# A Fourier mixer and a mixture of experts in one kernel: x loaded once per tile, and the first three batches' filter product without an exchange of rows on ScalarE

## The chip, the core and the metric

The kernel runs on one core of a Trainium2 chip. The metric is the device time of one execution in microseconds; the kernel before was timed three times.

## What is computed

The input x has 8 batches of 2496 tokens of 256 numbers, all in float32. Each batch is transformed along the tokens, multiplied by a complex filter, and transformed back. The result goes, token by token, to one of eight experts (the largest of eight logits), each with two matrices.

```python
X = np.fft.rfft(x, axis=1)
F = (filt_r + 1j * filt_i)[None, :, :]
y = np.fft.irfft(X * F, n=x.shape[1], axis=1)
x = y.reshape(B * S, D)
expert_idx = np.argmax(x @ w_gate, axis=1)
for e in range(E):
    h = np.maximum(x_sorted[lo:hi] @ w1[e], 0.0)
    y_sorted[lo:hi] = h @ w2[e]
return gate_w[:, None] * y_sorted[inv_perm]
```

## The kernel before, in words

The length 2496 is 39 times 64, so a transform is taken in stages, each a set of small matrix products on TensorE. For each batch:

- `add_x` (L378, L379): of a loaded tile of x, the sum `xs` of two halves and, in place, their difference. The sum is on GpSimd (POOL in the profile), the difference on VectorE (DVE) in batch 0 and on GpSimd in all others.
- Stage a (`stage_a`, L389; in batch 0 `first_a`, L472): the transform over 39, in six chunks. The result goes to DRAM (`zd`) and comes back in another layout as five tiles `z` (in batch 0 it stays on the core and is turned by TensorE, `turn_z`, L485).
- Stage b (`stage_b`, L403): the transform over 64. Its result lies in two PSUM banks `po`, with real parts in some rows and imaginary parts in others. Then the filter: VectorE makes `ys = po * hr` (L408), ScalarE (ACT) copies `po` to `yw` with the rows exchanged in blocks of 32, eight copies (L410), VectorE multiplies `yw` by `hi` (L411), and GpSimd adds the two (L412). `hi` carries signs that GpSimd puts into it once (L283).
- Stage c (`stage_c`, L424; in batch 0 `first_c`, L495): the way back over 64, from `ys`. The result goes to DRAM (`ud`) and comes back as tiles `u`.
- Stage d (`stage_d`, L445), the logits (L533) and `route`, which writes each token's row by an indirect DMA from GpSimd (L649), 22 per batch in groups of eight, eight and six, to a place that its expert owns.

The experts' tiles (`hidden`, L787, and `result`, L801) take those rows when enough are there, and fill TensorE between the stages and to the end.

The program is written as one list. `slot(k)` lists the steps of a slot: stages b and c of batch k, `add_x` and stage a of batch k+1, and stage d and routing of batch k-1. Each step has a place in its slot, a planned cost on TensorE and, where it needs one, the tile that has to be loaded. The loop at the end takes steps and expert work in turn, by these costs. `either` gives a copy out of PSUM to VectorE or ScalarE, whichever is planned free first. Every engine then works in the order in which its instructions were written; all loads and stores but the indirect ones stand in one queue, SyncE's (SP).

What is loaded, and in which order, comes from the steps too:

```python
todo = [step[2] for step in STEPS if step[2] and step[2] != "y"]
```

Both `add_x` and stage a of a chunk name the same tile of x, so each tile of x stands in `todo` twice and is loaded twice, into two of the seven buffers named `fin`.

Of the kernel before, what the change touches and what calls it, by code (L numbers as in the profile page):

```python
# [19 lines left out]
P = 128  # L20
# [37 lines left out]
def dft_tables():  # L58
# [29 lines left out]
    tc = tc.reshape(2, N2, N2)  # L88
    tc0 = np.zeros((2, N2, 2, 2, N2))
    for e in range(2):  # L90
        tc0[e, :, :, e] = tc.transpose(1, 0, 2)
# [13 lines left out]
    for e in range(2):  # L105
# [6 lines left out]
        "tc": np.concatenate([tc, tc], axis=1).transpose(1, 0, 2),  # L112
        "tc0": tc0.reshape(P, 2, P),
# [40 lines left out]
def kernel(  # L154
# [64 lines left out]
    tcs = cst.tile([P, 2, N2], F32, name="tcs")  # L219
# [20 lines left out]
    tc0 = pro.tile([P, 2, P], F32, name="tc0", bufs=1)  # L240
# [32 lines left out]
    HP = P // 2  # L273
    CH = [(i0, min(4, NG - i0)) for i0 in range(0, NG, 4)]
# [97 lines left out]
    def add_x(b, c):  # L372

        m = CH[c][1] // 2
        xt = ins["x", b, c]
        xs = xss[b, c] = sb.tile([TP, 2, D], F32, tag="xs", name="xs", bufs=2)
        lo, hi_ = xt[:TP, :m], xt[:TP, m:2 * m]
        nc.gpsimd.tensor_tensor(xs[:, :m], lo, hi_, op=ALU.add)  # L378
        (nc.vector if b == 0 else nc.gpsimd).tensor_tensor(hi_, lo, hi_, op=ALU.subtract)  # L379
        free["p"] = max(free["p"], now[0]) + (1.3 if b == 0 else 2.6)  # L380
# [15 lines left out]
    def stage_b(b, q):  # L396
# [9 lines left out]
        yw = sb.tile([P, 2, 2 * D], F32, tag="yw", name="yw", bufs=2)  # L406
        for o in range(2):
# [9 lines left out]
    def stage_c(b, q):  # L417
        ys = outs.pop(("y", b, q))
        uo = sb.tile([P, 4, D], F32, tag="st", name="uo", bufs=4)
        pe = [bank(), bank()]  # L420
        for o in range(2):
            for e in range(2):
                rows = slice(e * HP, (e + 1) * HP)
                mm(pe[e][o * HP:(o + 1) * HP, :], lhsT=tcs[rows, o, :], rhs=ys[rows, o, :], start=True, stop=True)  # L424
# [64 lines left out]
    def first_c(q):  # L489
        ys = outs.pop(("y", 0, q)).rearrange("p o (j d) -> p o j d", j=2)  # L490
        for h in range(DH):
            p = bank().rearrange("p (j o x) -> p j o x", j=2, o=2)
            for j in range(2):
                for o in range(2):
                    mm(p[:, j, o], lhsT=ys[:, o, j, h * P:(h + 1) * P], rhs=tc0[:, o, :], start=True, stop=True)  # L495
# [55 lines left out]
    def route(b, g):  # L551
# [13 lines left out]
        oh = small("oh", w, E)  # L565
# [42 lines left out]
        run = small("run", E, w, rows=P)  # L608
# [6 lines left out]
        pos = small("pos", E, w)  # L615
# [203 lines left out]
    def slot(k):  # L819

        steps, nch = [], len(CH)
        if k == 0:
            steps.append((0.4, load_rest, None, 0.0))
            for q in range(-1, NQ + 1):
# [58 lines left out]
    todo = [step[2] for step in STEPS if step[2] and step[2] != "y"]  # L883
# [145 lines left out]
```

## Time and profile before

| | |
|---|---|
| median of 3 runs | 1778.66 us (1776.59 to 1780.38) |
| the profiled execution | 1764.16 us |
| its span, first to last instruction | 1762.4 us |
| TensorE matmuls | 1577.6 us busy, 90% of the span |
| TensorE weight loads | 1059.7 us, 60% |
| ScalarE | 635.0 us, 36% |
| GpSimd | 556.2 us, 32% |
| VectorE | 458.3 us, 26% |

The profile is of one execution. Busy shares are means over stages with different limits, so they are read by stretches of time. A pass is one matmul as the trace records it: each float32 matmul of the program is two passes.

### The profile page before, as it was taken

The numbers are of one execution on the slowest core, as the hardware profiler recorded it, in microseconds if no ns is written. First come the engines' busy times: TensorE is split into PE (matmuls) and PEld (weight loads), VectorE is DVE, ScalarE is ACT, GpSimd is POOL, SyncE is SP. The second block draws the span as 40 slices with busy tenths as digits, with TensorE's granted clock in tenths as the row PEclk, the third lists the DMA queues.
The fourth block names the chain that finished last, engine by engine and source line by source line (L and its number), as shares of the span: only waits on it lengthen the run. The fifth ranks groups of instructions, "written<-read, shape, count | busy, mean of one in ns | idle before, by whom it ended". The sixth has DMA issues, their size and how long they took to land.

```text
span 1762.4 us, 22497 instructions
## 1 busy us (share of the span) xinstructions
PE 1577.6 (90%) x7058; PEld 1059.7 (60%) x7058; DVE 458.3 (26%) x1490; ACT 635.0 (36%) x1382; POOL 556.2 (32%) x498
## 2 busy tenths in 40 slices
PE   6785657579987989999997999999999999999998
PEld 4441224248552656565662675666767668889998
DVE  3554455531344421421124312111300000000000
ACT  3454443343453422533235433222222222223333
POOL 5535444444344342521223323112511111111111
PEclk9787668789997989999998999999999999999999
DMA  9457866486978264863537436333444445665561
GB/s 368 154 157 226 232 226 206 131 270 205 267 259 253 87 232 137 244 193 110 151 97 180 153 110 182 122 105 112 146 152 160 149 143 186 198 231 157 179 182 57
DMA packets 139238, 313.27 MB, mean 178 GB/s; under 512 B 21871, under 2 KB 62992, under 8 KB 139121
## 3 DMA queue, kind: packets, MB, share of 16 engines
q1 hardware_dynamic: 119905, 268.50, 49.8%
q0 software_dynamic: 19216, 43.33, 7.2%
q8 instruction: 58, 0.95, 0.2%
q14 instruction: 59, 0.48, 0.1%
HBM read 231.75 MB, written 80.90 MB: 177 GB/s over the span
## 4 chain that ended last, share of the span: by engine, by line
PE 72%; ACT 3%; DVE 3%; DMA 2%; issue 2%; POOL 2%; SPq 0%; POOLq 0%; DVEq 0%; ACTq 0%
PE bank L801 31%; PE bank L787 30%; ACT yw L410 3%; PE bank L445 2%; PE bank L780 2%; PE bank L389 2%; PE bank L519 1%; PE lt L533 1%; PE bank L403 1%; POOL rows L649 1%; DMA fin<-in_x_dram 1%; PE bank L424 1%; DMA w2t<-in_moe_w_dram 1%; DVE ys L408 0%; POOL xs L378 0%
## 5 line engine op out<-in xcount | busy, mean ns | idle before, releaser
L787 PE MATMUL bank<-xT,w1t 128*128 128x512 f32 (+2 forms) x2080 | 597.2, 441 | 17.0 <-issue 13.3
L801 PE MATMUL bank<-w2t,hT 128*128 128x256 f32 x2240 | 496.5, 380 | 2.1 <-ACT yw L410 1.3
L787 PEld LDWEIGHTS bank<-xT,w1t 128*128 128x128 f32 x2080 | 341.8, 193 | 242.7 <-issue 209.6
L801 PEld LDWEIGHTS bank<-w2t,hT 128*128 128x128 f32 x2240 | 421.1, 190 | 65.9 <-issue 6.6
L807 POOL DMA_INDIRECT out_dram<-ys,idt x163 | 161.2, 989 | 790.6 <-ACT ys L806 438.5
L791 ACT ACTIVATE hT<-bank 128x512 f32<-128x512 f32 (+2 forms) x500 | 217.1, 436 | 337.7 <-PE bank L787 337.5
L806 ACT ACTIVATE ys<-bank,gts 128x256 f32<-128x256 f32 x155 | 73.4, 474 | 491.4 <-PE bank L801 445.4
L649 POOL DMA_INDIRECT rows<-yo,row x176 | 176.5, 1003 | 171.3 <-DVE cnt L630 73.1
L410 ACT COPY yw<-bank 32x512 f32<-32x512 f32 x320 | 184.3, 576 | 100.5 <-DVE ys L408 96.7
L266 DVE COPY xT<-bank 128x512 f32<-128x512 f32 (+2 forms) x60 | 28.3, 475 | 543.6 <-PE bank L780 451.7
L412 POOL TENSOR_TENSOR ys<-ys,yw 128x1024 f32<-128x1024 f32 x40 | 94.0, 2349 | 171.1 <-DVE yw L411 126.8
L389 PE MATMUL bank<-xs,tas 117*120 117x512 f32 (+1 forms) x84 | 48.9, 668 | 67.7 <-POOL xs L378 38.7
L411 DVE TENSOR_TENSOR yw<-yw,hi 128x1024 f32<-128x1024 f32 x40 | 51.5, 1287 | 167.3 <-ACT yw L410 150.3
L801 PE MATMUL bank<-w2s,hT 128*128 x368 | 83.3, 379 | 0.0
L445 PE MATMUL bank<-fin,tds 120*117 120x512 f32 (+1 forms) x154 | 78.8, 631 | 0.1
L378 POOL TENSOR_TENSOR xs<-fin 117x512 f32<-117x512 f32 (+1 forms) x48 | 56.6, 1180 | 58.2 <-PE bank L389 31.1
L801 PEld LDWEIGHTS bank<-w2s,hT 128*128 128x128 f32 x368 | 68.2, 190 | 8.3
L408 DVE TENSOR_TENSOR ys<-bank,hr 128x512 f32<-128x512 f32 x80 | 51.4, 684 | 80.3 <-PE bank L403 78.7
L424 PE MATMUL bank<-ys,tcs 64*64 64x512 f32 x280 | 42.5, 680 | 30.3 <-POOL ys L412 30.3
L389 PEld LDWEIGHTS bank<-xs,tas 117*120 117x120 f32 x84 | 14.9, 208 | 85.8 <-POOL xs L378 71.6
L449 DVE TENSOR_TENSOR yo<-bank,even 117x256 f32<-117x256 f32 x88 | 37.1, 422 | 75.7 <-ACT even L448 73.2
L519 PEld LDWEIGHTS bank<-ident,yo 117*128 117x128 f32 x352 | 41.1, 150 | 25.1 <-issue 16.2
(134 smaller groups left out, 1092.7 us busy)
## 6 DMA issues: line engine op xcount, KB each, us to landing
w1t<-in_moe_w_dram SPq DMA_DIRECT2D x130, 512.0 KB, 3.9
w2t<-in_moe_w_dram SPq DMA_DIRECT2D x84, 512.0 KB, 4.8
fin<-in_x_dram SPq DMA_DIRECT2D x80, 512.0 KB, 6.0
fin<-zd SPq DMA_DIRECT2D x140, 128.0 KB, 5.2
ud<-uo SPq DMA_DIRECT2D x140, 128.0 KB, 3.0
zd<-zo SPq DMA_DIRECT2D x70, 240.0 KB, 5.6
fin<-ud SPq DMA_DIRECT2D x70, 240.0 KB, 5.8
xg<-rows SPq DMA_DIRECT2D x28, 544.0 KB, 4.6
```

The costliest lines, as they stand in the source:

```text
L389: mm(p, lhsT=tas, rhs=v, start=True, stop=True)
L410: nc.scalar.copy(out=yw[r:r + HB, o], in_=po[o][r ^ HB:(r ^ HB) + HB])
L412: nc.gpsimd.tensor_tensor(ys, ys, yw, op=ALU.add)
L424: mm(pe[e][o * HP:(o + 1) * HP, :], lhsT=tcs[rows, o, :], rhs=ys[rows, o, :], start=True, stop=True)
L445: mm(p[:TP, :], lhsT=tds[:k, :], rhs=uv[:, i], start=True, stop=True)
L519: nc.tensor.transpose(pt[:, 2 * i + dh, :TP], yo[:, j + i, dh * P:(dh + 1) * P], ident[:TP, :TP])
L649: sc = nc.gpsimd.indirect_dma_start(out=rowsd, out_offset=bass.IndirectOffsetOnAxis(ap=at, axis=0), in_=what, in_offset=None,)
L787: mm(p[:, :m], lhsT=w1t[2 * i + k // FH2][:, dh, k % FH2 * P:(k % FH2 + 1) * P], rhs=xts[i][:, dh, :m], start=(dh == 0), stop=(dh == DH - 1))
L791: lambda: nc.scalar.activation(hT[:, :m], p[:, :m], AF.Relu))
L801: mm(p[:, :D], lhsT=hs[i][k][:, j * P:(j + 1) * P], rhs=w2, start=(k == 0), stop=(k == FT - 1))
L806: lambda: nc.scalar.activation(ys, p[:, :D], AF.Copy, scale=gate))
L807: nc.gpsimd.indirect_dma_start(out=out, out_offset=bass.IndirectOffsetOnAxis(ap=idt[i].bitcast(U32)[:, j, :], axis=0), in_=ys, in_offset=None,
```

## The change

It does three things, and leaves batches 3 to 7 as they were but for the loads and one place in the list.

- `todo` keeps each tile once, so x is loaded 48 times, not 96.
- In batches 0 to 2 (`EARLY = 3`), `add_x` is on VectorE whole. In every batch its place in the list moves from 0.1 to 0.05 of a slot ahead of stage a.
- In batches 0 to 2, stage b's result is multiplied twice by VectorE, `ys = po * hr` and `yw = po * hi`, without any exchange; stage c then takes both products into the same PSUM bank, with two matrices, the second being the first with its two halves of rows exchanged and its sign turned. ScalarE's eight copies, VectorE's multiplication of `yw`, and GpSimd's addition are gone there.

```diff
+    tc = np.stack([tc, -tc[:, ::-1]], axis=1).reshape(2, 2, N2, N2)
...
+    EARLY = 3
...
-        nc.gpsimd.tensor_tensor(xs[:, :m], lo, hi_, op=ALU.add)
-        (nc.vector if b == 0 else nc.gpsimd).tensor_tensor(hi_, lo, hi_, op=ALU.subtract)
-        free["p"] = max(free["p"], now[0]) + (1.3 if b == 0 else 2.6)
+        eng = nc.vector if b < EARLY else nc.gpsimd
+        eng.tensor_tensor(xs[:, :m], lo, hi_, op=ALU.add)
+        eng.tensor_tensor(hi_, lo, hi_, op=ALU.subtract)
...
+        if b < EARLY:
+
+            for o in range(2):
+                for y, h in ((ys, hr), (yw, hi)):
+                    nc.vector.tensor_mul(y[:, o], po[o], h[:, q, 2 * o:2 * o + 2].rearrange("p j d -> p (j d)"))
+            outs["w", b, q] = yw
+            free["v"] = max(free["v"], now[0]) + 2.8
+            return
...
-                mm(pe[e][o * HP:(o + 1) * HP, :], lhsT=tcs[rows, o, :], rhs=ys[rows, o, :], start=True, stop=True)
+                for i, y in enumerate(parts):
+                    mm(pe[e][o * HP:(o + 1) * HP, :], lhsT=tcs[rows, o, i, :], rhs=y[rows, o, :],
+                       start=(i == 0), stop=(i == len(parts) - 1))
...
-                    mm(p[:, j, o], lhsT=ys[:, o, j, h * P:(h + 1) * P], rhs=tc0[:, o, :], start=True, stop=True)
+                    for i, y in enumerate(parts):
+                        mm(p[:, j, o], lhsT=y[:, o, j, h * P:(h + 1) * P], rhs=tc0[:, o, i, :], start=(i == 0), stop=(i == 1))
...
-                    steps.append((at + 0.02, lambda q=q: first_c(q - 1), None, 1.7))
+                    steps.append((at + 0.02, lambda q=q: first_c(q - 1), None, 3.4))
...
-                    steps.append((at + 0.01, lambda q=q: stage_c(k, q - 1), None, 0.95))
+                    steps.append((at + 0.01, lambda q=q: stage_c(k, q - 1), None, 1.8 if k < EARLY else 0.95))
...
-                steps.append((at - 0.1, lambda c=c: add_x(k + 1, c), ("x", k + 1, c), 0.0))
+                steps.append((at - 0.05, lambda c=c: add_x(k + 1, c), ("x", k + 1, c), 0.0))
...
-    todo = [step[2] for step in STEPS if step[2] and step[2] != "y"]
+    todo = list(dict.fromkeys(step[2] for step in STEPS if step[2] and step[2] != "y"))
```

The routing's small tiles `oh`/`run` and `ex`/`pos` now share buffers, which makes room for the larger matrices.

How the order of instructions moves, at three places. First SyncE's queue at the start of the program, before:

```order
L964 DMA tas<-in_ta_dram 117x120
L355 DMA fin<-in_x_dram 128x1024 x9
L355 DMA fin<-in_x_dram 128x512
L355 DMA fin<-in_x_dram 128x1024
L355 DMA fin<-in_x_dram 128x512
L355 DMA fin<-in_x_dram 128x1024
L279 DMA sgs<-in_sg_dram 128x20
```

and now:

```order
L982 DMA tas<-in_ta_dram 117x120
L358 DMA fin<-in_x_dram 128x1024 x5
L358 DMA fin<-in_x_dram 128x512
L358 DMA fin<-in_x_dram 128x1024
L282 DMA sgs<-in_sg_dram 128x20
L283 DMA tbs<-in_tb_dram 128x64
```

Thirteen loads of x stood ahead of the filter's tables; seven do now.

Second, VectorE in batch 0, around stage b's first two tiles (`zi`, `zo`, `ut` are copies out of PSUM), before:

```order
L408 TENSOR_TENSOR ys<-bank,hr 128x512 x2
L411 TENSOR_TENSOR yw<-yw,hi 128x1024
L266 COPY zi<-bank 128x512 x2
L266 COPY zo<-bank 120x512
L408 TENSOR_TENSOR ys<-bank,hr 128x512 x2
L411 TENSOR_TENSOR yw<-yw,hi 128x1024
```

and now:

```order
L418 TENSOR_TENSOR ys<-bank,hr 128x512
L418 TENSOR_TENSOR yw<-bank,hi 128x512
L418 TENSOR_TENSOR ys<-bank,hr 128x512
L418 TENSOR_TENSOR yw<-bank,hi 128x512
L382 TENSOR_TENSOR xs<-fin 117x512
L383 TENSOR_TENSOR fin<-fin 117x512
L418 TENSOR_TENSOR ys<-bank,hr 128x512
```

The multiplication that waited for ScalarE is gone, the copies that stood behind it went to ScalarE, and batch 1's sums stand between the products.

Third, GpSimd around batch 3's sums (`rows` are the indirect writes of batch 0's tokens), before:

```order
L412 TENSOR_TENSOR ys<-ys,yw 128x1024 x2
L378 TENSOR_TENSOR xs<-fin 117x512
L379 TENSOR_TENSOR fin<-fin 117x512
L649 DMA rows<-yo,row 160768x272 x7
L378 TENSOR_TENSOR xs<-fin 117x512
```

and now:

```order
L286 TENSOR_TENSOR hi<-hi,sgs 128x1024 x5
L667 DMA rows<-yo,row 160768x272 x8
L382 TENSOR_TENSOR xs<-fin 117x512
L383 TENSOR_TENSOR fin<-fin 117x512
L667 DMA rows<-yo,row 160768x272 x8
L382 TENSOR_TENSOR xs<-fin 117x512
```

Batch 3's first sum stands behind eight writes and its second behind eight more; no addition of `ys` and `yw` is left between them.

## Rows read from the trace of the kernel before

**Rows 1.** The page's first line.

```profile
span 1762.4 us, 22497 instructions
```

**Rows 2.** Windows: PE, PEld, DVE, ACT and POOL busy, granted clock, DMA share, GB/s.

```profile
0.00:24.40 24.40, 14.18 (x96) 13.47 (x96) 8.75 (x24) 5.94 (x14) 8.69 (x22) 1.00 0.91 333
24.40:81.00 56.60, 39.64 (x177) 23.61 (x177) 29.20 (x39) 27.75 (x47) 34.97 (x22) 0.81 0.60 219
81.00:163.50 82.50, 57.10 (x268) 25.84 (x271) 37.88 (x82) 41.44 (x81) 35.83 (x27) 0.79 0.64 194
163.50:255.80 92.30, 57.61 (x237) 23.98 (x229) 48.09 (x142) 41.85 (x86) 39.81 (x33) 0.70 0.75 228
...
1000.00:1762.40 762.40, 755.87 (x3540) 573.90 (x3538) 76.03 (x382) 227.94 (x567) 151.71 (x154) 1.00 0.48 152
```

**Rows 3.** Waits of PE, whole span: us in total, times, longest.

```profile
PE bank L389 <- POOL xs L378: 38.7, 7, 13.3
PE bank L424 <- POOL ys L412: 30.3, 6, 8.5
...
PE bank L403 <- DVE zi L266: 10.8, 4, 3.3
...
PE bank L495 <- POOL ys L412: 4.4, 1, 4.4
```

**Rows 4.** Timeline of PE, start and slot 0: start, us, instruction, idle before it.

```profile
9.56 2.06 PE L472 MATMUL bank<-tas,xs 117*128 117x120 f32 x8 [9.56 <-POOL seg L303]
...
33.49 2.57 PE L403 MATMUL bank<-zi,tbs 64*64 64x512 f32 x8 [3.34 <-DVE zi L266]
...
46.04 1.95 PE L495 MATMUL bank<-tc,ys 128*128 128x128 f32 x16
```

**Rows 5.** Timeline of VectorE, the product behind the exchange.

```profile
158.00 1.22 DVE L411 TENSOR_TENSOR yw<-yw,hi 128x1024 f32<-128x1024 f32 x1 [4.17 <-ACT yw L410]
```

**Rows 6.** Timeline of PE, slots 1 and 2.

```profile
120.82 1.03 PE L424 MATMUL bank<-ys,tcs 64*64 64x512 f32 x8
...
147.26 1.99 PE L424 MATMUL bank<-ys,tcs 64*64 64x512 f32 x8 [6.86 <-POOL ys L412]
...
150.18 1.06 PE L389 MATMUL bank<-fin,tas 117*120 117x256 f32 x2
...
161.79 1.98 PE L424 MATMUL bank<-ys,tcs 64*64 64x512 f32 x8 [8.52 <-POOL ys L412]
...
174.75 1.99 PE L424 MATMUL bank<-ys,tcs 64*64 64x512 f32 x8 [4.71 <-POOL ys L412]
176.66 3.04 PE L445 MATMUL bank<-fin,tds 120*117 120x512 f32 x4
184.35 2.06 PE L389 MATMUL bank<-xs,tas 117*120 117x512 f32 x2 [4.66 <-POOL xs L378]
...
204.42 2.06 PE L389 MATMUL bank<-xs,tas 117*120 117x512 f32 x2 [10.95 <-DMA ud<-uo]
```

**Rows 7.** Groups by line: operation, count, busy us, mean ns, idle before.

```profile
L408 DVE TENSOR_TENSOR ys<-bank,hr 128x512 f32<-128x512 f32 x80 | 51.4, 684 | 80.3 <-PE bank L403 78.7 <-issue 0.9 <-POOL xs L378 0.4
...
L379 DVE TENSOR_TENSOR fin<-fin 117x512 f32<-117x512 f32 (+1 forms) x6 | 4.4, 730 | 10.7 <-POOL xs L378 10.7
```

**Rows 8.** Stage c's line alone, 120.7 to 121.9 us: durations, first and last start.

```profile
L424 PE MATMUL bank<-ys,tcs x8: 589/590/591, 120.8 to 121.3; 64*64 64x512 f32 x8
```

**Rows 9.** Timeline of GpSimd in slot 2.

```profile
194.33 1.00 POOL L649 DMA_INDIRECT rows<-yo,row  x1 [8.68 <-DVE cnt L630]
...
203.09 1.27 POOL L378 TENSOR_TENSOR xs<-fin 117x512 f32<-117x512 f32 x1
```

**Rows 10.** DMA issues: count, KB each, median us to landing.

```profile
fin<-in_x_dram SPq DMA_DIRECT2D x80, 512.0 KB, 6.0
fin<-zd SPq DMA_DIRECT2D x140, 128.0 KB, 5.2
```

**Rows 11.** The chain that ended last, 420 to 700 us: start, us.

```profile
460.88 6.38 DMA fin<-in_x_dram
```

More of the change, by code (lines that the diff above doesn't have):

```diff
@@ L87, in dft_tables @@
         tc[o, 0, :, 1], tc[o, 1, :, 1] = sn.T, cs.T
-    tc = tc.reshape(2, N2, N2)
-    tc0 = np.zeros((2, N2, 2, 2, N2))
+    tc = np.stack([tc, -tc[:, ::-1]], axis=1).reshape(2, 2, N2, N2)
+    tc0 = np.zeros((2, N2, 2, 2, 2, N2))
     for e in range(2):
-        tc0[e, :, :, e] = tc.transpose(1, 0, 2)
+        tc0[e, :, :, :, e] = tc.transpose(2, 0, 1, 3)
     ids = np.zeros((NB, N1, NG))
@@ L111, in dft_tables @@
         "tb": tb.reshape(P, N2),
-        "tc": np.concatenate([tc, tc], axis=1).transpose(1, 0, 2),
-        "tc0": tc0.reshape(P, 2, P),
+        "tc": np.concatenate([tc, tc], axis=2).transpose(2, 0, 1, 3),
+        "tc0": tc0.reshape(P, 2, 2, P),
         "td": td.reshape(TK, TP),
@@ L218 @@
     tbs = cst.tile([P, N2], F32, name="tbs")
-    tcs = cst.tile([P, 2, N2], F32, name="tcs")
+    tcs = cst.tile([P, 2, 2, N2], F32, name="tcs")
     tds = cst.tile([TK, TP], F32, name="tds")
@@ L239 @@
     pro = first.enter_context(tc.tile_pool(name="pro", bufs=2, side="right"))
-    tc0 = pro.tile([P, 2, P], F32, name="tc0", bufs=1)
+    tc0 = pro.tile([P, 2, 2, P], F32, name="tc0", bufs=1)
     pools = {}
@@ L377, in add_x @@
         lo, hi_ = xt[:TP, :m], xt[:TP, m:2 * m]
-        nc.gpsimd.tensor_tensor(xs[:, :m], lo, hi_, op=ALU.add)
-        (nc.vector if b == 0 else nc.gpsimd).tensor_tensor(hi_, lo, hi_, op=ALU.subtract)
-        free["p"] = max(free["p"], now[0]) + (1.3 if b == 0 else 2.6)
+        eng = nc.vector if b < EARLY else nc.gpsimd
+        eng.tensor_tensor(xs[:, :m], lo, hi_, op=ALU.add)
+        eng.tensor_tensor(hi_, lo, hi_, op=ALU.subtract)
+        if b < EARLY:
+            free["v"] = max(free["v"], now[0]) + 1.4
+        else:
+            free["p"] = max(free["p"], now[0]) + 2.6
     def stage_a(b, c):
@@ L406, in stage_b @@
         yw = sb.tile([P, 2, 2 * D], F32, tag="yw", name="yw", bufs=2)
+        if b < EARLY:
+            for o in range(2):
[4 more added lines that the diff above has]
+            return
         for o in range(2):
@@ L417, in stage_c @@
     def stage_c(b, q):
-        ys = outs.pop(("y", b, q))
+        parts = [outs.pop((y, b, q)) for y in ("yw" if b < EARLY else "y")]
         uo = sb.tile([P, 4, D], F32, tag="st", name="uo", bufs=4)
@@ L489, in first_c @@
     def first_c(q):
-        ys = outs.pop(("y", 0, q)).rearrange("p o (j d) -> p o j d", j=2)
+        parts = [outs.pop((y, 0, q)).rearrange("p o (j d) -> p o j d", j=2) for y in "yw"]
         for h in range(DH):
@@ L564, in route @@
         nc.vector.tensor_reduce(mx, lg, axis=AX.X, op=ALU.max)
-        oh = small("oh", w, E)
+        oh = small("oh", w, E, rows=P)[:TP]
         ex = small("ex", w, E)
@@ L607, in route @@
             yield
-        run = small("run", E, w, rows=P)
+        run = small("run", E, w, rows=P, tag="oh")
         runf = run.rearrange("p e t -> p (e t)")
@@ L613, in route @@
         yield
-        pos = small("pos", E, w)
+        pos = small("pos", E, w, tag="ex")
         posf = pos.rearrange("p e t -> p (e t)")
```

## The prediction
> **What bounds the kernel now.** I read the page first: TensorE is 90% busy, and no other engine passes 36%. That is a mean, so next come the windows [rows 2]. From 1000 us to the end TensorE is busy 755.87 of 762.40 us at the full granted clock: the experts' work stands there and nothing hides it. In the first 256 us it is busy only 14.18, 39.64, 57.10 and 57.61 us of stretches of 24.4, 56.6, 82.5 and 92.3 us, and after the first stretch its clock is granted at 0.81, 0.79 and 0.70, a mix of 1.2 and 2.4 GHz after many idle spells. There are few rows for the experts yet. So the end moves with TensorE's own work, which the change raises, and with its idle time early, which the change is to lower: an early microsecond saved moves all that follows.
>
> Then the waits of TensorE [rows 3] say for what it sits idle: x's sums on GpSimd, GpSimd's addition of `ys` and `yw` (30.3 us before stage c, 4.4 before its form in batch 0), and `zi`, a copy by VectorE (10.8 us). The last is one cause seen from another engine: VectorE, in order, stands 4.17 us before its product with `hi` until ScalarE's eight copies are done [rows 5], and the copies of `zi` stand behind it. The timelines [rows 4, 6] say where these waits lie: in slots 0 to 2, but for part of x's sums.
>
> Below about 0.2%, 3.6 us, a measurement of this kernel can't be told from no change.
>
> **Start.** The first matmul comes at 9.56 us [rows 4]. The tile it needs is the third load of x in the queue and will be the first. In that stretch DMA moved 333 GB/s [rows 2], and a load is 512 KB [rows 10]: 1.6 us each, so up to 3.1 us earlier. The sum on VectorE takes about 0.73 us [rows 7] where GpSimd takes 1.27 [rows 9]. I take 3 us; bounds 0 (the loads share the engines) and 4.
>
> **Slot 0.** TensorE idles 17.0 of 56.6 us [rows 2]; the waits for `zi` and for `ys` make 15.2 of it [rows 3] and lose their cause. In its place batch 0's stage c takes 16 more passes, five times, at 1.95 us [rows 4]: 9.8 us more. VectorE has per step four products at 0.684 us and 1.2 pairs of sums at 0.73 [rows 7], 4.5 us, within a step of about 10 us, so it is no bound. Net 5.4 us. TensorE stays busy more evenly, and its 39.64 us at 0.81 would be 7.5 us shorter at full clock; I count 3 of them. Together 8.4; bounds 0 (new waits as long as half of the old) and 13.
>
> **Slot 1.** Two waits for GpSimd's addition, 6.86 and 8.52 us [rows 6]. The first goes whole. Behind the second comes batch 2's stage b, which needs `z`, loaded after the slot's last stage a has been stored. That stage a ends at 151.2 us [rows 6]; a small store and then a load at 5.2 us [rows 10], with the issue of both, end near 159.5, where stage b begins at 163.55 now. So 4 us of the second wait go and the rest becomes a wait for `z`. Saved 10.9.
>
> Against that stands stage c, eight passes more, now five times in the slot. Its eight passes take 1.03 us at the full clock and 1.99 at the lower one [rows 6]; one pass lasts 590 ns [rows 8], so one after the other they would take 4.7. Four run at a time, one in each 64 by 64 quadrant, in two rounds 0.44 us apart (1.03 less the last pass's 0.59). Two more rounds are 0.88 us at the full clock and twice that at the lower; I take 1.3. The bound below is 0.88, the bound above eight passes that overlap nowhere, 4.7 us. Four of five lie on the path, 5.2 us. Net 5.7; bounds -5 and 11.
>
> **Slot 2.** Stage c's wait of 4.71 us goes. The wait of 4.66 for batch 3's sum goes too: GpSimd did that sum behind an addition which is gone. The 10.95 us at 204.42 [rows 6] are x's sum behind seven of the indirect writes [rows 9], each some 1.3 us from the one before. The sums of batch 3 stay on GpSimd, and the order now has eight writes ahead of the second of them; but the ranks that release the writes now stand on TensorE ahead of batch 1's last stage b, so that the writes start while TensorE waits for `z`. I count half, 5.5 us. Stage c costs 6.5. New is a wait for `u`: it is read at 176.66, 12.9 us after batch 1's last stage c ended [rows 6], over a store and a load that the change doesn't shorten. Of the 12.9 us TensorE now works 8.2 and waits the 4.71 that go; 1.3 of these are filled by stage c's new passes, 3.4 become a wait for `u`. Net 4.9; bounds -8 and 14.
>
> **Loads once.** Half of x's loads go, 40 of 512 KB and 8 of half that, 22 MB, and in SyncE's queue the loads behind them stand that much earlier. The seven buffers hold seven tiles in use, not pairs. Later in the trace the chain passes through a load of x, 6.38 us [rows 11]. I count 5 us for slots 3 to 5; bounds 0 (hidden anyway) and 15.
>
> In slot 1 VectorE gains six pairs of sums, 8.8 us at most, and five times two products of 0.684 in place of one of 1.22 [rows 5, 7], 0.7 us. They lie beside TensorE (VectorE is busy 37.88 of 82.50 us there [rows 2]); without that cover they would cost their 9.5 us. Sums for batch 3 and later are written nearer to their stage a; where GpSimd is at indirect writes, that may cost some of the later waits of 38.7 us [rows 3] again, and is rival two.
>
> **Sum:** 3 + 8.4 + 5.7 + 4.9 + 5 = 27 us off the profiled execution's 1764.16 us (span 1762.4 [rows 1]), 1737 us. That execution ran 14.5 us under the median of the three runs; I take the same amount off the median 1778.66, and predict 1752 us.
>
> **Rivals.** *One: the quadrants hold each other up.* The program now gives each quadrant its four passes in a row, `ys` and `yw`, two passes each, before the next quadrant's first. If a pass can't begin before those ahead of it in the program have begun, only the last pass of one quadrant and the first of the next overlap: 13 rounds in place of 2. A round is 0.44 us at the full clock and twice that at the lower, so ten stage c's cost 7 us more each, not 1.3: 57 us, and the kernel takes 1752 + 57 = 1809 us. With some room to look past a stalled pass it is about 4 us more each, 1790. It decides from 4 us per stage c (1.3 + 27/10). Against it speaks that today's order is already two passes per quadrant in a row, and that by the same rule they would take five rounds, 4 x 0.44 + 0.59 = 2.35 us at the full clock, where the row shows 1.03. I give it 0.1. The Trainium skill ("TensorE: Matmul & The Clock Gate", part 3, on packing small matmuls) states that rule: matmuls start and end strictly in program order, even on different tiles of the array. Rows 6 and 8 of this case disagree with it for two passes; no run here shows four.
>
> *Two: the gain is taken back later.* What arrives sooner waits for x's sums behind indirect writes in slots 2 to 4, where the longest wait is 13.3 us now [rows 3], and for the experts' first rows. Four waits more of the mean size, 38.7/7 = 5.5 us, 22 us, leave 1774 us. For it: the later lead of `add_x`. Against it: the order behind slot 2 is nearly what it was. 0.17.
>
> *Three: the clock comes back.* The 57.10 and 57.61 us at 0.79 and 0.70 [rows 2] would be 12 and 17 us shorter at the full clock. If even spells without idle time regain most of it, 25 us more go: 1727 us. 0.15.
>
> That the change doesn't do what it says is excluded by the order: one load per tile, and no copies by ScalarE.
>
> **Numbers.** Forecast 1752 us (own range 1737 to 1765), 0.58; rival three 0.15, two 0.17, one 0.10. The range reaches to rivals two and three, with a few us for the bounds: 1722 to 1776. Faster by over 0.2%: all of the first two and three quarters of rival two, 0.86. Within 0.2%: 0.04. Slower: rival one, 0.10.
>
> **What would show it.** Right: no wait of TensorE for `zi` or for `ys` in slots 0 to 2; stage c's 16 passes in about 1.9 us at the full clock; the first matmul near 6.5 us; batch 3's stage b (255.80 now, with which slot 2 ends) some 20 us earlier; idle time left at 204 us, in front of `z` and `u`. Wrong: stage c's passes at 4 us or more, or slot 3 beginning earlier but the last 760 us not.

## The result, and the profile after

The changed kernel takes 1689.23 us (median of 4 runs, 1687.10 to 1692.92) where the kernel before took 1779.52 us (4 runs on the same chip): a ratio of 0.9496, 95% interval 0.9472 to 0.9520. It is 90 us or 5.0% faster. Forecast were 1752 us (1722 to 1776): the sign was right, the gain was more than three times the one forecast, and the time lies below the range.

Later runs of the kernel before took 1764.21 us (median of 7) on one chip and 1777.60 to 1779.62 us on others. The profile of before (1764.16 us) fits the first, the profile after (1691.03 us) was taken with the second. So the two traces differ by 73 us and not by 90, and every experiment is judged by its ratio to the kernel before on its own chip; 0.01 is 17.8 us. The difference between chips lies late. From batch 7's first stage b to the end, a second profile of before took 835.0 us on the faster chip (931.86 to 1766.9); the six experiments below that leave all from batch 3 on as it was written took 842.6 to 845.1 us there on others. In slot 4 they took 162.0 to 164.4 us, the two profiles of before 158.1 and 160.0. Slots 0 to 2 can be compared.

The page of the changed kernel, span and busy time (share, instructions):

```profile
span 1689.3 us, 22545 instructions
...
PE 1571.4 (93%) x7218; PEld 1064.3 (63%) x7218; DVE 438.2 (26%) x1480; ACT 594.0 (35%) x1317; POOL 487.3 (29%) x453
```

TensorE has 160 passes more than before (7058) and is busy 6 us less in all. Its windows, cut where the slots now end (columns as in [rows 2]):

```profile
0.00:19.70 19.70, 13.16 (x98) 12.70 (x98) 8.76 (x20) 8.46 (x24) 3.67 (x18) 1.00 0.91 346
19.70:59.70 40.00, 37.40 (x257) 26.56 (x257) 21.89 (x36) 19.39 (x27) 7.49 (x4) 1.00 0.58 200
59.70:121.40 61.70, 54.17 (x314) 27.28 (x316) 40.09 (x109) 25.20 (x55) 10.83 (x10) 0.92 0.67 192
121.40:197.70 76.30, 57.55 (x288) 26.43 (x280) 32.67 (x119) 25.33 (x58) 38.20 (x36) 0.82 0.88 270
```

Against [rows 2] the slots are 40.0, 61.7 and 76.3 us long where they were 56.6, 82.5 and 92.3, and the granted clock is 1.00, 0.92 and 0.82 where it was 0.81, 0.79 and 0.70. TensorE's idle time in the three went from 77.1 to 28.9 us; its busy time, with the extra passes in it, from 154.4 to 149.1.

Its waits now (answering [rows 3]):

```profile
PE bank L440 <- POOL ys L427: 17.6, 4, 10.1
PE bank L396 <- issue: 12.4, 2, 8.9
PE lt L551 <- ACT yt L267: 11.5, 3, 8.7
...
PE bank L396 <- POOL xs L382: 3.7, 1, 3.7
```

The waits for `ys` that are left all belong to batch 3 and later; those for `zi` are gone but for 0.2 us; the 38.7 us for x's sums on GpSimd are 3.7, though batches 3 to 7 still have them there. One more such wait hides in the second line, under "issue" (its releaser is not in the records). GpSimd's timeline early in slot 2 shows it:

```profile
122.03 1.00 POOL L667 DMA_INDIRECT rows<-yo,row  x1 [13.18 <-DVE row L647]
...
131.07 0.99 POOL L667 DMA_INDIRECT rows<-yo,row  x1 [0.30 <-issue]
132.08 1.27 POOL L382 TENSOR_TENSOR xs<-fin 117x512 f32<-117x512 f32 x1
```

```profile
133.40 2.06 PE L396 MATMUL bank<-xs,tas 117*120 117x512 f32 x2 [8.92 <-issue]
```

Eight indirect writes stand between batch 3's first sum, at 106 us, and its second, the one shown; TensorE's stage a waits 8.92 us and begins at 133.40, as the sum ends. The timeline of TensorE shows the start, two stages b of batch 0 with a stage c between them (its first two pieces), a stage c of batch 1, and batch 3's first stage b (answering [rows 4, 6]):

```profile
5.89 2.06 PE L489 MATMUL bank<-tas,xs 117*128 117x120 f32 x8 [5.89 <-DVE xs L382]
...
33.75 1.09 PE L410 MATMUL bank<-zi,tbs 64*64 64x512 f32 x8
...
35.70 0.39 PE L513 MATMUL bank<-tc,ys 128*128 128x128 f32 x2
35.92 0.39 PE L513 MATMUL bank<-tc,yw 128*128 128x128 f32 x2
...
41.08 1.09 PE L410 MATMUL bank<-zi,tbs 64*64 64x512 f32 x8
...
89.15 1.10 PE L440 MATMUL bank<-ys,tcs 64*64 64x512 f32 x8
90.01 1.10 PE L440 MATMUL bank<-yw,tcs 64*64 64x512 f32 x8
...
197.73 1.09 PE L410 MATMUL bank<-fin,tbs 64*64 64x512 f32 x8
```

The first matmul comes at 5.89 us. A step of batch 0, from one stage b to the next, takes 7.33 us; before it took about 10. Stage c's sixteen passes in batch 1 end 1.96 us after their first begins.

### The profile page after: what moved, and what is told of

Same layout as the page of the kernel before. It is cut to its first block, busy times and chain, and to the rows that moved or that the text cites. A ratio compares the mean times of both kernels' runs of the same rounds, so it can differ in the third digit from the quotient of the medians.

```text
span 1689.3 us, 22545 instructions
## 1 busy us (share of the span) xinstructions
PE 1571.4 (93%) x7218; PEld 1064.3 (63%) x7218; DVE 438.2 (26%) x1480; ACT 594.0 (35%) x1317; POOL 487.3 (29%) x453
## 3 DMA queue, kind: packets, MB, share of 16 engines
q1 hardware_dynamic: 112993, 245.63, 48.2%
## 4 chain that ended last, share of the span: by engine, by line
PE 85%; DVE 5%; issue 3%; ACT 3%; DMA 2%; POOL 1%; SPq 0%; POOLq 0%; DVEq 0%; ACTq 0%
PE bank L819 33%; PE bank L805 33%; PE bank L462 4%; PE bank L396 3%; PE bank L410 2%; ACT yw L425 2%; PE bank L798 2%; PE bank L440 2%; PE bank L537 2%; PE lt L551 1%; PE bank L513 1%; PE bank L489 1%; POOL rows L667 1%; DVE ys L423 0%; POOL ys L427 0%
## 5 line engine op out<-in xcount | busy, mean ns | idle before, releaser
L425 ACT COPY yw<-bank 32x512 f32<-32x512 f32 x200 | 115.2, 576 | 54.1 <-DVE ys L423 40.3
L427 POOL TENSOR_TENSOR ys<-ys,yw 128x1024 f32<-128x1024 f32 x25 | 58.8, 2350 | 134.7 <-DVE yw L426 107.1
L396 PE MATMUL bank<-xs,tas 117*120 117x512 f32 (+1 forms) x84 | 45.1, 621 | 28.0 <-issue 12.4
L426 DVE TENSOR_TENSOR yw<-yw,hi 128x1024 f32<-128x1024 f32 x25 | 30.8, 1234 | 103.5 <-ACT yw L425 82.7
L798 PEld LDWEIGHTS bank<-ident,xg 128*128 128x128 f32 x326 | 39.2, 143 | 25.2 <-issue 22.7
L798 PE MATMUL bank<-ident,xg 128*128 128x128 f32 x326 | 47.4, 277 | 7.0 <-issue 6.5
L537 PE MATMUL bank<-ident,yo 117*128 117x117 f32 x352 | 47.7, 279 | 6.2 <-ACT yw L425 2.8
```

The source lines that it names most:

```text
L396: mm(p, lhsT=tas, rhs=v, start=True, stop=True)
L425: nc.scalar.copy(out=yw[r:r + HB, o], in_=po[o][r ^ HB:(r ^ HB) + HB])
L537: nc.tensor.transpose(pt[:, 2 * i + dh, :TP], yo[:, j + i, dh * P:(dh + 1) * P], ident[:TP, :TP])
L798: nc.tensor.transpose(pt[:, j, :], xg[:, j, dh * P:(dh + 1) * P], ident)
```

## The experiments

All in one table; below, what each was to tell. "After" is the changed kernel.

| kernel | ratio to before | 95% interval |
|---|---|---|
| after | 0.9496 | 0.9472 to 0.9520 |
| before + loads once | 0.9867 | 0.9837 to 0.9896 |
| before + two products | 0.9689 | 0.9664 to 0.9713 |
| before + sums on VectorE (batches 0 to 2) | 1.0062 | 1.0043 to 1.0082 |
| after, exchange as before | 0.9969 | 0.9954 to 0.9983 |
| after, loads twice | 0.9677 | 0.9660 to 0.9694 |
| after, sums on GpSimd | 0.9478 | 0.9449 to 0.9506 |
| after, old place of `add_x` | 0.9492 | 0.9475 to 0.9510 |
| before + stage c's passes twice | 1.0016 | 1.0003 to 1.0029 |
| before + stage c's passes four times | 1.0121 | 1.0100 to 1.0142 |
| before, no addition on GpSimd | 0.9824 | 0.9808 to 0.9840 |
| before, no exchange on ScalarE | 0.9728 | 0.9708 to 0.9748 |
| before + loads once, five buffers | 0.9868 | 0.9852 to 0.9885 |
| after, batches 0 to 3 | 0.9390 | 0.9374 to 0.9407 |
| after, batches 0 to 4 | 0.9237 | 0.9211 to 0.9263 |
| after, all batches | 0.9183 | 0.9167 to 0.9199 |
| after, products in all batches | 0.9261 | 0.9242 to 0.9280 |
| after, sums in all batches | 0.9669 | 0.9649 to 0.9690 |

### One part alone

**Loads once.**

```diff
-    todo = [step[2] for step in STEPS if step[2] and step[2] != "y"]
+    todo = list(dict.fromkeys(step[2] for step in STEPS if step[2] and step[2] != "y"))
```

> The kernel before with one part of the change alone: each tile of x is loaded once. The whole change measured 90 us shorter. Theory one (the chain of ScalarE's exchange and GpSimd's addition held TensorE up, and more than its named waits went with it): loads alone give 0 to 10 us, a time of 1770 to 1780. Theory two (the loads: half of x's transfers gone from SyncE's queue, and seven buffers that hold seven tiles and not pairs, so that x and the z and u behind it come sooner all through slots 0 to 4): 30 us or more, below 1750. Theory three (x's sums on GpSimd, which stood between indirect writes and additions, were the longest waits): 0 to 10 us, since the sums stay where they were.

25.8 us shorter (1753.83 against 1779.62): between what the theories gave, and five times my term. TensorE's waits for x's sums on GpSimd, 38.7 us before [rows 3], are nearly gone, and so are GpSimd's own waits for x's loads, 24.1 us before. In this kernel:

```profile
PE bank L389 <- POOL xs L378: 3.5, 1, 3.5
```

```profile
POOL xs L378 <- DMA fin<-in_x_dram: 3.2, 1, 3.2
```

and GpSimd's in the kernel before:

```profile
POOL xs L378 <- DMA fin<-in_x_dram: 24.1, 6, 8.5
```

The one is not the other's cause, though: by the timelines GpSimd's waits for loads lie up to 18 us, at 86 and at 467 us (one of 0.5 us later), TensorE's for sums mostly at 264, 312 and 563 us (6.17, 13.29 and 10.94). There the sum comes straight behind indirect writes. The longest, in the kernel before, on GpSimd and on TensorE:

```profile
309.98 0.98 POOL L649 DMA_INDIRECT rows<-yo,row  x1 [0.30 <-issue]
310.98 1.27 POOL L378 TENSOR_TENSOR xs<-fin 117x512 f32<-117x512 f32 x1
```

```profile
312.31 2.06 PE L389 MATMUL bank<-xs,tas 117*120 117x512 f32 x2 [13.29 <-POOL xs L378]
```

With loads once the same sum, batch 4's fourth, comes ahead of these eight writes, with 30 of the writes before it and not 38, and TensorE doesn't wait for it:

```profile
278.99 1.30 POOL L378 TENSOR_TENSOR xs<-fin 117x512 f32<-117x512 f32 x1
```

```profile
288.81 1.12 PE L389 MATMUL bank<-xs,tas 117*120 117x512 f32 x2
```

So this edit did more than take loads away. In the two traces TensorE, VectorE and ScalarE work through the same instructions in the same order; GpSimd's order changed. The section on the kernel before says that every engine works in the order written; the kernel asks for that (`manual_schedule`) on TensorE, VectorE, ScalarE and SyncE, and GpSimd is not among them. How much of the 25.8 us is this order and how much the loads, no run shows.

**The two products** (the stage b, stage c, `first_c` and matrix parts of the diff ahead; loads and sums as before).

> The kernel before with the two products and the second matrix alone, in batches 0 to 2; x is loaded twice and its sums stay on GpSimd. Theory one: 50 to 65 us shorter, 1715 to 1730, with batch 3's stage b at about 215 us (255.80 before, 197.7 with the whole change) and no wait of TensorE for zi or ys in slots 0 to 2. Theory two: 10 to 25 us shorter, the waits for ys turning into waits for z, u and x. Theory three: 10 to 25 us, with x's sums behind what GpSimd still does as the longest waits left in slots 1 and 2.

56 us shorter, as theory one has it, with batch 3's stage b at 210.06 us and no wait over 0.3 us for `zi` or `ys` in slots 0 to 2:

```profile
210.06 1.09 PE L406 MATMUL bank<-fin,tbs 64*64 64x512 f32 x8
```

What it leaves, 18.2 us in 6 waits for x's sums on GpSimd, lies mostly later (2.8 us of it before 210 us), so theory three falls here too.

**The sums.**

```diff
-        nc.gpsimd.tensor_tensor(xs[:, :m], lo, hi_, op=ALU.add)
-        (nc.vector if b == 0 else nc.gpsimd).tensor_tensor(hi_, lo, hi_, op=ALU.subtract)
+        eng = nc.vector if b < 3 else nc.gpsimd
+        eng.tensor_tensor(xs[:, :m], lo, hi_, op=ALU.add)
+        eng.tensor_tensor(hi_, lo, hi_, op=ALU.subtract)
...
```

> The kernel before with x's sums of batches 0 to 2 on VectorE alone; ScalarE's exchange, GpSimd's addition and the double loads stay. Theory one: 0 to 10 us shorter, 1770 to 1780, since the chain stays (VectorE, which has the two products with an exchange between them, only gets more to do; a loss of some us is possible). Theory two: 0 to 5 us. Theory three: 30 us or more, below 1750.

0.6% slower: theory three falls, and the loss is one that theory one only allowed for.

**The change without its products** (both edits above, and the new place of `add_x`).

> The change without its two products: loads once, sums on VectorE in batches 0 to 2, sums at the later place, and ScalarE's exchange with GpSimd's addition as before. Theory one: 20 to 35 us shorter than the kernel before (1745 to 1760), so that the products are worth 55 to 70 us on top. Theory two or three: 65 to 80 us shorter (1700 to 1715), so that the products are worth 10 to 25. If the parts need each other (each wait has two causes, and taking one away only shows the other), this run and the one with the products alone add up to clearly less than the 90 us of the whole.

Only 5.5 us shorter, below all three theories; with the products alone that makes 62 of the 90 us, as expected for parts that need each other. Beside the exchange the sums, at their new place, eat up 20 of the 25.8 us that loads once give. The trace shows how. VectorE, two steps in slot 1:

```profile
157.03 2.55 DVE L379 TENSOR_TENSOR xs<-fin 117x512 f32<-117x512 f32 x1
...
164.46 1.29 DVE L412 TENSOR_TENSOR ys<-bank,hr 128x512 f32<-128x512 f32 x2 [4.16 <-PE bank L407]
169.93 1.23 DVE L415 TENSOR_TENSOR yw<-yw,hi 128x1024 f32<-128x1024 f32 x1 [4.18 <-ACT yw L414]
171.07 1.28 DVE L266 COPY uo<-bank 128x512 f32<-128x512 f32 x2
172.27 1.68 DVE L379 TENSOR_TENSOR xs<-fin 117x256 f32<-117x256 f32 x1
```

and GpSimd beside it, and TensorE behind it:

```profile
156.69 2.34 POOL L416 TENSOR_TENSOR ys<-ys,yw 128x1024 f32<-128x1024 f32 x1 [5.29 <-DVE yw L415]
171.32 2.34 POOL L416 TENSOR_TENSOR ys<-ys,yw 128x1024 f32<-128x1024 f32 x1 [12.29 <-DVE yw L415]
```

```profile
174.00 1.21 PE L393 MATMUL bank<-xs,tas 117*120 117x256 f32 x2 [8.80 <-DVE xs L379]
```

```profile
PE bank L393 <- DVE xs L379: 51.1, 8, 8.9
```

The sum stands in VectorE's queue behind the product with `hi`, which waits 4.18 us for ScalarE's copies. TensorE waits 8.80 us for the sum, 51.1 us in 8 such waits in all. So the sums on VectorE cost time as long as the exchange is there; the products don't need them.

### One part taken back

**Loads twice again.** `todo` as before, all else as changed.

> The changed kernel (1689.2 us) with each tile of x loaded twice again, all else as changed. Loads once gave 25.8 us alone in the kernel before. If the parts add up, this is 20 to 30 us slower than the changed kernel, 1709 to 1719. If loads once only took away what the other two parts take away too (waits with two causes), it is 0 to 12 us slower, 1689 to 1701. If the loads are worth more once TensorE is faster early, because the queue of loads then becomes the bound, it is over 30 us slower.

By ratio 1.8% slower than after, 32 us with an uncertainty of about 7: the parts add up. GpSimd's order moved with the loads here too. Whether loads once are worth more in company than the 25.8 us alone, the intervals don't tell.

**Sums on GpSimd again** (the old `add_x`, at the new place).

> The changed kernel with x's sums on GpSimd again (in batch 0 the difference on VectorE, as in the kernel before). Measured so far: the sums on VectorE alone cost 8.7 us, and 20 us on top of loads once, while products alone (-56.3) and loads once alone (-25.8) add up to 82 of the 90 us. Theory one: the sums on VectorE cost only while VectorE's queue stands before its product with hi for ScalarE's copies; without the exchange they gain. Then this kernel is 5 to 20 us slower than the changed one, 1694 to 1709. Theory two: the sums on VectorE cost in any company, and the later place of add_x or chance in the order makes up the rest. Then it is 5 to 15 us faster, 1674 to 1684, and would beat the change.

0.9478 against 0.9496: no difference that the intervals tell. Neither theory; with the exchange gone, the sums of batches 0 to 2 cost and gain nothing on either engine.

**The old place of `add_x`.**

```diff
-                steps.append((at - 0.05, lambda c=c: add_x(k + 1, c), ("x", k + 1, c), 0.0))
+                steps.append((at - 0.1, lambda c=c: add_x(k + 1, c), ("x", k + 1, c), 0.0))
```

> The changed kernel with add_x at its old place in the list, 0.1 of a slot ahead of stage a and not 0.05. Theory one: the place only says which instructions stand ahead of the sums; in batches 0 to 2 VectorE comes to them in time either way. Within 5 us of the changed kernel, 1684 to 1694. Theory two: the place is worth what the sums seem to cost, since a sum that stands early in an engine's queue waits for its load and holds up what is behind it; 8 to 20 us slower, 1697 to 1709.

0.9492, no difference: theory one. So the whole gain is the products and loads once, 3.1 and 1.3% alone, 5.2% together (the run with the sums on GpSimd).

**The kernel before, profiled again.**

> The kernel before once more, for a second profile: the first profiled execution took 1764.16 us, some 15 us less than the median of its runs, while those of the other kernels stand within 5 us of theirs. If executions of this kernel differ in the early slots (waits that fall one way or the other), a profile near 1779 us shows batch 3's stage b later than 255.8 us. If they differ later, in the experts' part or by the granted clock there, it begins at the same time, and the last 760 us are longer.

1768.68 us where its 7 neighbours had a median of 1764.21, with batch 3's stage b at 254.31 us. Neither reading: that profile was not odd, the chip was another.

### Inside the products

**Stage c's passes twice**, with exchange and addition in place (in `first_c` likewise).

```diff
-                mm(pe[e][o * HP:(o + 1) * HP, :], lhsT=tcs[rows, o, :], rhs=ys[rows, o, :], start=True, stop=True)
+                for i in range(2 if b < 3 else 1):
+                    mm(pe[e][o * HP:(o + 1) * HP, :], lhsT=tcs[rows, o, :], rhs=ys[rows, o, :], start=True, stop=True)
```

> The kernel before with every matmul of stage c issued twice in batches 0 to 2 (the second writes the same numbers over the first): the change's extra passes and nothing else of it. The prediction charged 21.5 us for them (9.8 in batch 0, 5.2 and 6.5 in batches 1 and 2, before the clock). Theory one, as predicted: the passes lie on the path, 12 to 22 us slower, 0.7 to 1.2% over the kernel before. Theory two: they cost next to nothing, because TensorE works more evenly and is granted a higher clock, so that each pass beside it is shorter, and because some of them fill waits: within 5 us, 0.3%, or even faster, with a granted clock over the 0.81, 0.79 and 0.70 of slots 0 to 2.

0.16% slower, 2.9 us: theory two. Its windows of slots 0 to 2:

```profile
24.80:81.00 56.20, 43.39 (x250) 30.39 (x247) 28.33 (x39) 27.75 (x47) 35.15 (x22) 0.88 0.60 216
81.00:163.40 82.40, 58.03 (x319) 26.44 (x322) 38.82 (x82) 41.54 (x81) 36.51 (x27) 0.87 0.66 199
163.40:257.90 94.50, 63.88 (x276) 26.72 (x268) 48.08 (x142) 41.89 (x85) 40.43 (x33) 0.72 0.75 223
```

In slots 0 and 1 there are 73 and 51 passes more than in [rows 2], and the slots are not longer. TensorE is busy 3.75 and 0.93 us more, at a granted clock of 0.88 and 0.87 where it was 0.81 and 0.79. In slot 2, with 39 more, the clock hardly rose (0.72 and 0.70) and the slot is 2.2 us longer. GpSimd's order moved here too, at one of x's sums.

**Four times** (`range(4 ...)` in both places).

> The kernel before with every matmul of stage c issued four times in batches 0 to 2 (the same numbers written again). Issued twice it cost 0.16%, 2.9 us, where I had charged 21.5 us. Theory one (the passes fill time in which TensorE waits, and raise the clock): the first doubling was nearly free because the idle time and the low clock took it up; four times is three such steps, 32 passes more per stage c, some 3.9 us each at the full clock in batch 0 and 1.8 us or more in batches 1 and 2, and the cover runs out in part: 0.5 to 1.5%, 9 to 27 us. Theory two (the passes cost what their rounds take, and 2.9 us was an early gain elsewhere): three times the charge, 40 us and more, over 2.2%.

1.21%, 21.5 us: theory one. The first doubling costs 2.9 us, the two further steps of the same size 18.6 together; in the kernel before, the cover is about as large as the passes that the change adds.

**No addition on GpSimd.** Stage c takes `ys` and the exchanged `yw` with the same matrix.

```diff
-        nc.gpsimd.tensor_tensor(ys, ys, yw, op=ALU.add)
+        if b < 3:
+            outs["w", b, q] = yw
+            return
+        nc.gpsimd.tensor_tensor(ys, ys, yw, op=ALU.add)
...
+                for i, y in enumerate(parts):
+                    mm(pe[e][o * HP:(o + 1) * HP, :], lhsT=tcs[rows, o, :], rhs=y[rows, o, :],
+                       start=(i == 0), stop=(i == len(parts) - 1))
```

> The kernel before, in batches 0 to 2 without GpSimd's addition of ys and yw: stage c takes both into the same bank with the same matrix, after ScalarE's exchange as before. The products alone, which remove the exchange and the addition, gave 3.1%, 55 us. Theory one: GpSimd's addition is what TensorE waited for, since it stands in GpSimd's queue behind x's sums and the indirect writes; 35 to 55 us shorter, 2 to 3.1%. Theory two: ScalarE's eight copies are the long link, some 4.6 us of each step, and VectorE's queue stands behind them; then this gives 0 to 15 us, under 0.9%. If the links simply stand one behind the other, 20 to 30 us.

1.76%, 31 us, 1 us above the range for links one behind the other and under that of theory one, so nearest to the links one behind the other; this kernel has the change's extra passes in it.

**No exchange on ScalarE.** Both products from the bank as it is, the addition stays. The kernel leaves the exchange of rows out, so its numbers are not the filter's product; TensorE has as many passes as before (7058).

```diff
+        if b < 3:
+            for o in range(2):
+                for y, h in ((ys, hr), (yw, hi)):
+                    nc.vector.tensor_mul(y[:, o], po[o], h[:, q, 2 * o:2 * o + 2].rearrange("p j d -> p (j d)"))
+            nc.gpsimd.tensor_tensor(ys, ys, yw, op=ALU.add)
...
+            return
```

> The kernel before, in batches 0 to 2 without ScalarE's exchange of rows (both products come from the bank as it is, so that the filter's product is computed without its exchange); GpSimd adds them as before and stage c takes one product. Theory one (the addition): 0 to 15 us shorter, under 0.9%, with the waits of stage c for ys on GpSimd near the 30 us they had. Theory two (the exchange, and VectorE's queue behind it): 35 to 55 us, 2 to 3.1%. One behind the other: 20 to 30 us.

2.72%, 48 us: theory two, and the two links add up to 79 us where both together gave 56, so some of the time goes with either. The 48 us lie in slots 0 to 2; up to batch 2's first stage b, and on to batch 3's:

```profile
24.10:125.50 101.40, 79.15 (x445) 41.39 (x449) 50.88 (x104) 41.03 (x75) 68.72 (x47) 0.95 0.83 264
125.50:206.90 81.40, 51.12 (x236) 21.59 (x231) 43.13 (x140) 22.68 (x52) 40.34 (x32) 0.79 0.81 249
```

These are 182.8 us where [rows 2] have 231.4. About half of the gain is idle time (77.1 to 52.5 us). The other half is TensorE's busy time, 154.4 to 130.3 us with as many passes as before (681 and 682), at a granted clock of 0.95 and 0.79 where it was 0.81, 0.79 and 0.70.

Two more rows tell the two links apart in batch 0. Its stages b in this kernel:

```profile
36.75 1.09 PE L403 MATMUL bank<-zi,tbs 64*64 64x512 f32 x8
...
43.51 1.07 PE L403 MATMUL bank<-zi,tbs 64*64 64x512 f32 x6
```

and in the one without the addition:

```profile
34.29 2.57 PE L403 MATMUL bank<-zi,tbs 64*64 64x512 f32 x8 [5.23 <-DVE zi L266]
...
44.39 1.58 PE L403 MATMUL bank<-zi,tbs 64*64 64x512 f32 x8 [0.69 <-DVE zi L266]
```

A step is 6.76 us without the exchange and 10.10 with it. In batch 0 the exchange sets the step, through VectorE's queue and `zi`; the addition does not. Without the exchange nine of the ten copies of `zi` also stand on ScalarE, where VectorE had them, so the two rows show both together.

### The loads

**Five buffers**, and each tile loaded once.

```diff
-    NIN = 7
+    NIN = 5
```

> The kernel before with each tile of x loaded once, and five buffers fin in place of seven. Loads once with seven buffers gave 1.33%, 25.8 us, alone and 1.8% in the company of the other parts, where the prediction took 5 us and 3 at the start. Theory one (the buffers): before, SyncE's queue stands at a load until one of the seven buffers is free (27.7 us in 7 waits for stage a, 15.7 and 19.0 for others), with the stores and loads of z and u behind it, because x's tiles take two each; with five buffers that comes back, and 15 us or more of the gain go (ratio 0.994 or more). Theory two (the bytes and the entries in the queue): the 22 MB that are not moved stay away, so the ratio stays within 0.3% of 0.9867.

0.9868: nothing lost, theory one falls. SyncE's queue, at loads of x, in this kernel:

```profile
SPq L355 <- PE bank L403: 18.7, 8, 6.9
...
SPq L355 <- PE bank L389: 15.8, 4, 6.9
```

It stands there for a buffer again, 34.5 us by these two lines (35.5 in the kernel before, 8.3 with seven buffers and loads once), and the time does not change. GpSimd's order is again another than before: batch 4's fourth sum has 30 writes ahead of it and comes at 282.79. What is left is this order, the load's place in the queue, and the 22 MB not moved; no run tells the three apart.

### In which batches

`EARLY` is the number of batches that have both parts.

> The changed kernel with the two products and the sums on VectorE in batch 3 too. In the changed kernel the longest waits for ys left, 17.6 us in 4, belong to batches from 3 on, and the clock is still granted at 0.73 from 250 to 300 us. If what held batches 0 to 2 up holds batch 3 up too, 5 to 20 us shorter than the change (ratio to the kernel before 0.939 to 0.947). If by then the experts' tiles fill TensorE, the extra passes cost and nothing comes back: 0 to 5 us slower (0.950 to 0.953).

> The changed kernel with the two products and the sums on VectorE in batches 0 to 4. With batches 0 to 3 the ratio was 0.939. If the chain over ScalarE and GpSimd still holds TensorE up in batch 4, 3 to 12 us more: 0.932 to 0.937. If the experts' tiles fill TensorE by then (no waits in the last 760 us before), the passes cost and nothing comes back: 0.939 to 0.942.

> The changed kernel with the two products and the sums on VectorE in all batches. If the chain costs only where TensorE has no expert work, batches 5 to 7 add 15 stage c's of eight passes, each 0.88 us at the full clock, 13 us, 0.7%, on top of what batches 0 to 4 give: 0.940 to 0.947. If the chain still holds up something there (ScalarE and GpSimd also serve the experts' results), it is level with or below batches 0 to 4.

0.9390, 0.9237 and 0.9183: each gains, four batches as much as expected at most, five more than expected, and eight go on gaining, as the second reading there has it. With all batches the kernel takes 1634.5 us where before takes 1779.1 and is 3.3% faster than the change. I had thought that the experts' tiles cover batches 5 to 7. Windows of the changed kernel:

```profile
450.00:600.00 150.00, 136.14 (x552) 79.81 (x553) 57.00 (x167) 61.01 (x121) 66.01 (x54) 0.94 0.61 184
600.00:1000.00 400.00, 381.72 (x1577) 235.28 (x1576) 111.73 (x351) 148.07 (x290) 127.16 (x112) 0.98 0.51 149
```

and of the one with all batches:

```profile
450.00:600.00 150.00, 149.54 (x633) 95.50 (x635) 23.38 (x86) 41.55 (x83) 29.47 (x30) 1.00 0.46 145
600.00:1000.00 400.00, 392.04 (x1671) 240.48 (x1662) 103.98 (x379) 114.32 (x233) 92.10 (x94) 0.99 0.52 154
```

Some 32 us of idle time stood between 450 and 1000 us in the changed kernel, and 8 are left.

**One part in all batches.** `add_x` on VectorE for `b < 3` with the products everywhere, and the other way round.

> The changed kernel with the two products in all eight batches, the sums of x on VectorE in batches 0 to 2 only. Both parts in all batches gave 0.9183, the change 0.9496. Theory one: the exchange and the addition make it, 0.918 to 0.925, as in batches 0 to 2, where taking the sums back to GpSimd changed nothing (0.9478). Theory two: from batch 3 on GpSimd has the indirect writes in its queue and x's sums behind them (waits of 13.3, 10.95 and 6.17 us before), so there the sums carry half or more: 0.930 to 0.945. With GpSimd's additions gone its queue would hold only sums and writes, which speaks for theory one.

> The changed kernel with x's sums on VectorE in all eight batches, the two products in batches 0 to 2 only. Sums on VectorE cost 0.6 to 1.0% in batches 0 to 2 as long as VectorE's queue also stands for ScalarE's exchange there. From batch 3 on it does here. Theory one (the sum stands behind that wait, one tile of x per step): 0 to 1.5% slower than the change, 0.950 to 0.964. Theory two (GpSimd's indirect writes are the longer queue from batch 3 on): faster than the change, 0.930 to 0.947.

Products in all batches 0.9261, just above the range of theory one and below that of theory two, so they are three quarters of the further gain (2.4 of 3.1%). Sums in all batches, without the products from batch 3 on, 0.9669, 1.7% slower than the change, past the upper end of theory one. TensorE's largest wait in that kernel is the one seen beside the exchange above:

```profile
PE bank L396 <- DVE xs L382: 62.4, 15, 9.8
```

On top of the products the sums gain 0.8% from batch 3 on (0.9261 to 0.9183). The part that loses everywhere beside the exchange gains there once the exchange is gone.

## Why the prediction was right, and why its size was wrong

By its own terms, from the two traces (stretches between stages b; the chip enters in slot 4 and at the end):

| term | forecast, us | traced, us |
|---|---|---|
| start | 3 | 4.8 |
| slot 0 | 8.4 | 16.6 |
| slot 1 | 5.7 | 20.8 |
| slot 2 | 4.9 | 16.0 |
| slots 3 to 5 | 5 | 23.5 |
| to the end | 0 | -8.5 (the chip's own difference is about that) |

In the row before the last, slot 4 is 6.2 us longer than before (164.3 against 158.1), within what other chips show where that slot is as it was (162.0 to 164.4).

**Right:** what bounds the kernel (idle time of the early slots, behind which everything moves); three of the five signs that "What would show it" named: no wait over 0.3 us for `zi` or `ys` in slots 0 to 2, the sixteen passes at 1.96 us against "about 1.9", the first matmul at 5.89 against 6.5. The other two were off: batch 3's stage b came 58 us earlier (197.73), not 20, and the idle time left stands before x's sum.

**The step that failed first: the extra passes as a charge.** In "Slot 0" 9.8 us were set against the gain and 3 given back for the clock; in slots 1 and 2, 5.2 and 6.5 were charged. That is 18.5 us net. Measured by itself the doubling costs 2.9 us. In the changed kernel TensorE's busy time in the three slots did not rise by 18.5 but fell by 5.2 (154.4 to 149.1): 23.7 of the 34.4 us by which slots 0 to 2 were missed. Duration and number of the passes were right, but they lay on the time that the waits freed, and the passes beside them ran at a granted clock of 1.00, 0.92 and 0.82. The run without the exchange, which has no extra passes, shows what the clock is worth: there the same passes take 24.1 us less than before. The row that said so was in the text: 39.64 us at 0.81 would be 7.5 us shorter, and I counted 3; for slots 1 and 2 the clock stood in a rival of its own, with 0.15. A stretch with waits in it and a mixed clock should be costed as a whole: idle time and slow passes go together.

**The second: only named waits were credited.** I took 37.6 us out of the slots' idle time, from the waits for `ys`, `zi` and x's sums. The idle time fell by 48.2. The rest are waits under other names, the largest of them 7.9 us for `av_i`, a small tile on VectorE, that are gone in these slots; that they stood behind the exchange is likely and not shown one by one.

**The third: "I count 5 us" for loads once.** The term was for slots 3 to 5; with loads once alone these are 19.6 us shorter (batch 3's first stage b at 249.99 us, batch 6's at 691.75). In all they measured 25.8 us alone and 32 in company (interval about 25 to 39); with the start counted in, I had 8. One reason given, seven buffers that hold no pairs, was wrong: five do as well. And the order behind slot 2 was taken as "nearly what it was". Of the 38.7 us in the first line of [rows 3], 30.4 stand in three waits behind indirect writes, and with loads once these sums come ahead of a group of writes.

**Sums on VectorE** were counted as part of the start and of two waits. They cost 0.6% alone and nothing in company. That they needed the other part I did not see; the 9.5 us "without that cover" was the right question asked of TensorE's time, not of VectorE's queue.

**The rivals.** One (quadrants hold each other up) is refuted by the rows at 89.15 and 90.01 us and by the doubled passes. The rule of the Trainium skill ("TensorE: Matmul & The Clock Gate", part 3), which gave it, disagrees with the trace now for four passes per quadrant as well as for two. Two (the gain taken back) has its mechanism in the trace, the 8.92 us behind eight indirect writes, but not its size: of slots 0 to 5 each is shorter than before but slot 4, whose 6.2 us more are within the difference between chips. That wait stands where a new one for `u` was forecast; none for `u` is among the larger ones. Three was nearest: the clock did come back, in slot 0 whole and in slots 1 and 2 in part, and its 1727 us was the closest of the four times. It needed no mechanism apart from the removed waits and so belonged into the sum.

What stays open: for the loads, GpSimd's order, place in the queue or bytes; and which waits beyond the named ones the exchange held up.

## What to carry to other kernels

Where an engine's clock stands at a mixed value and a stretch has waits, price a change there by the whole stretch: work added to the waiting engine may cost a small part of its duration (2.9 of 21.5 us here), and the waits removed give back more than their names say. Ask of each releaser what stood ahead of it in its own queue, and after an edit compare the order of every engine, not only of those that it names. Ask also of each instruction moved to another engine what waits stand ahead of it in that queue; the same move lost 1.7% without the other edit and gained 0.8% with it. And test where a change's reach ends: here the part that was kept to three batches was worth about as much again in the other five.

## What the runs showed of the hardware that was not expected

- Sixteen float32 passes of 512 columns on four 64 by 64 quadrants, four in a row in the program for each, take 1.96 us; one lasts 0.589 us.
- A sum of two tiles on VectorE, 693 ns in the median, took 2.55 us (157.03) beside GpSimd's addition, and ended 0.55 us after that one had. The Trainium skill ("GPSIMD Engine Reference", section 1, specifications) states that GpSimd shares its interfaces to the on-chip memory with VectorE instructions that read two tiles from it; this row agrees.
- The same kernel differs by 0.8 to 0.9% between chips (1764.21 against 1777.60 to 1779.62 us), and more than half of it, 8 to 10 us, lies in the last 840 us, in which TensorE is busy 814.74 of 835.00 us.
